# Attention through 32 landmarks with a two-layer feed-forward, one core: a shared PSUM slot for two output tiles, an earlier w_out load, and a first softmax by halves

## The chip, the core and the metric

The kernel runs on one core of a Trainium2 chip. The core has engines that run their own instruction streams side by side and wait for each other through semaphores: PE (TensorE, matmuls into the accumulation memory PSUM), ACT (ScalarE, functions of one tensor), DVE (VectorE, elementwise work), POOL (GpSimd, here used to start loads) and SP (SyncE, here used to start stores and transposing transfers). Sixteen DMA engines move the data. The metric is the device time of one execution in microseconds (us), as the median of several runs.

## The reference

For 8 batches of 8 heads, 576 tokens and 64 channels, a set of 32 landmark queries p first attends to k and v. The 32 results then serve as both keys and values for the 576 queries q. The outputs of the heads are joined to rows of 512, multiplied by w_in (512 x 2048), passed through a smooth ReLU, and multiplied by w_out (2048 x 512).

```python
def sm_attn(qq, kk, vv):
    s = scale * qq @ kk.T
    a = exp(s - max(s));  a = a / (sum(a) + 1e-9)
    return a @ vv
p_packed = sm_attn(p, k, v)                 # 32 x 64 for each head
x = join_heads(sm_attn(q, p_packed, p_packed))   # 4608 x 512
h = x @ w_in
g = where(h >= 1, h, where(h <= -1, 0, (h + 1)**2 / 4))
out = g @ w_out
```

## The kernel before

Loads cast float32 to bf16 on the way. Each batch b goes through these steps, named as the tiles are in the profile:

- k and q are turned (`tp`, `kT`, `qT`): in batches 0 and 1 by PE with copies out of PSUM, in later batches by transposing transfers that SP starts. The landmarks p are turned by PE (`tpp`, `pT`), for batches 2 to 7 in one step.
- PE multiplies landmarks with k (`sp`), ACT takes the exponent (`ex`), PE multiplies with v (`pk`), and the result is copied (`ppT`). From batch 2 on DVE first copies v into `vz`.
- PE multiplies the packed keys with q (`s`), ACT takes the exponent (`eT`), PE sums over the landmarks (`sm`), ACT makes the reciprocal as logarithm and exponent (`ln`, `rc`), and DVE scales (`A`). The eight heads go as two groups of four (`G = 2`).
- The packed values are multiplied with w_in at once (`mp`, copied to `M`, in four parts of 512 columns), so that a tile of the hidden layer (`h`, 128 of the 2048 columns, all 576 tokens as two halves) is four matmuls of M with A.
- The smooth ReLU of an h tile is three steps: `x` on ACT, `t` on DVE or ACT, `hT` on DVE.
- Two batches make a pair of 1152 tokens, which is nine output tiles of 128 tokens. An output tile (`o`) sums sixteen matmuls, one for each h tile; it is copied to `ob` by ACT or DVE and stored by SP.

The order of everything is made when the program is built. Each step is a `Task` with a rank, the engines that may run it with assumed durations, what it depends on, and what buffers it takes. `Plan.run` plays the tasks against these durations and always takes the step that can start first (within a slack, the one of the lowest rank); the instructions are emitted in that order, and on the chip each engine keeps to it. So a rank or an assumed duration that changes moves instructions on all engines.

PSUM holds three slots of two banks (buffer `w`, pool `psW`), through which nearly all tiles pass, and two slots of one bank (buffer `o`, pool `psO`) for output tiles. In the first pair of batches output tiles 2 and 5 borrow a `w` slot each (`LENT`). Until the first output matmul, gaps that the plan foresees on PE are filled with matmuls on zeros (`o<-zeros`, `warm`, line 866).

The loads of w_in and w_out come in quarters (`win0` to `win3`, `wout0` to `wout3`), in the order of `LOADS`. `wout0` is needed by the first four matmuls of every output tile. k and v of batches 2 to 7 each have one buffer (`kz`, `v`), so a batch's load waits until the batch before has used it.

Of the kernel before, what the change touches and what calls it, by code (L numbers as in the profile page):

```python
# [11 lines left out]
class Task:  # L12
# [4 lines left out]
    def __init__(self, rank, ways, deps=(), takes=(), mode=None, behind=()):  # L17
        self.rank, self.ways, self.deps = rank, ways, list(deps)
        self.behind = [d for d in behind if d is not None]
        self.takes, self.frees, self.mode = list(takes), [], mode  # L20
        self.start = self.end = self.engine = None
        self.users = []


class Plan:
# [7 lines left out]
    def __init__(self, buffers):  # L33
        self.tasks = []
# [5 lines left out]
    def add(self, rank, ways, deps=(), takes=(), mode=None, behind=()):  # L40
        t = Task(rank, ways, deps, takes, mode, behind)
        self.tasks.append(t)
        return t
# [7 lines left out]
    def run(self, slack):  # L51
# [6 lines left out]
        while ready:  # L58
            best = None
            found = defaultdict(list)  # L60
            left = {b: sorted(v) for b, v in self.slots.items()}
            for t in sorted(ready, key=lambda t: t.rank):
                at = max((d.end + self.LATENCY for d in t.deps), default=0.0)
                at = max([at] + [d.start + 0.001 for d in t.behind])
                need = defaultdict(int)
                for b in t.takes:
                    need[b] += 1
                short = any(len(left[b]) < n for b, n in need.items())
                wants = at < self.free["PE"] + self.CLAIM
                for b, n in need.items():  # L70
                    if not short:
                        at = max(at, left[b][n - 1] + self.LATENCY)
                    if wants:
                        del left[b][:n]
                if short:
                    continue
                for e in t.ways:
                    found[e].append((max(self.free[e], at), t))
            for e, some in found.items():
                first = min(x[0] for x in some)  # L80
                at, t = min((x for x in some if x[0] <= first + slack.get(e, 0.0)), key=lambda x: (x[1].rank, x[0]))
                if best is None or at < best[0]:
                    best = at, t, e
# [38 lines left out]
def kernel(  # L122
# [20 lines left out]
    P = 128  # L143
# [16 lines left out]
    XSPLIT = 0  # L160
    FROM, C5, R5 = 2, 5, 64
    PAIRED = 2
    SPLIT, AHALF, WPARTS, MPARTS, QLATE, ORDER3, ORDER, MERGE = 2, 0, 1, 2, 0, 4, 2, 2
    Q0 = [range(0, 8, 2), range(1, 5, 2), range(5, 9, 2)]
    LOADS = "k0 v0 q0 win0 win1 win2 k1 wout0 v1 wout1 win3 wout2 q1 wout3 q2 v2 k2 p"
# [3 lines left out]
    LENT = [2, 5]  # L169
# [22 lines left out]
    plan = Plan(dict(BUFS, dma=8))  # L192
# [64 lines left out]
    def dma(key, rank, emit, mb, takes=(), settle=0.9):  # L257
        t = plan.add(rank, {"DMA": (0.78, 2.1, emit, mb / 0.405, settle)}, takes=list(takes) + ["dma"])
# [22 lines left out]
    def load_five(nm, b, rank):  # L281

        for i, (c, p0, t0) in enumerate([(C5, 0, 0), (C5 - 1, R5, C5 * R5)]):
            def emit(e, c=c, p0=p0, t0=t0):
                of = {"k": k, "v": v}[nm][b, :, t0:t0 + R5 * c].rearrange("h (p c) d -> p h (c d)", c=c)
                G_.dma_start(tokens(nm, b)[p0:p0 + R5, :, :c * D], of)  # L286
            dma((nm, b, i), rank + 0.01 * i, emit, 1.3 * c / 9, [nm] if i == 0 else [], 0.9 if b < 2 else 1.7)
# [4 lines left out]
    def load(nm, b, rank):  # L292

        if five(nm, b):
            load_five(nm, b, rank)
            return
        for i, hs in enumerate({("k", 0): [range(4, 8)], ("q", 0): Q0}.get((nm, b), [range(H)])):
            def emit(e, hs=hs):
                G_.dma_start(tokens(nm, b)[:, heads(hs)], rows_of(nm, b, hs))  # L299
            mb = MB0.get((nm, b, hs[0]), (1.18 if b < 2 else 1.3) * len(hs) / H)  # L300
# [601 lines left out]
```

## Time and profile before

| what | value |
|---|---|
| runs (us) | 243.82, 243.79, 244.25; median 243.82 |
| profiled execution | 244.38 us, of which the span is 242.6 us |
| busy in the span | PE 236.0, ACT 196.0, DVE 176.4, weight loads 134.5, POOL 36.2 us |
| granted PE clock | full in every slice |
| moved by DMA | 36.24 MB, mean 149 GB/s |

The span runs from the first to the last instruction of the profiled execution; its own time has 1.78 us around that. A busy PE counts matmuls as they overlap, so it says that PE had no gap, not that it ran at its peak. A group row ends with the idle time of the engine just before the group and what ended it. A timeline row gives the start, the length, the engine, the line, the operation and the number of instructions that are merged into it. A row on DMA gives the queue, the size and the time from issue to landing.

### The profile page before, as it was taken

The numbers are of one execution on the slowest core, as the hardware profiler recorded it, in microseconds if no ns is written. First come the engines' busy times: TensorE is split into PE (matmuls) and PEld (weight loads), VectorE is DVE, ScalarE is ACT, GpSimd is POOL, SyncE is SP. The second block draws the span as 40 slices with busy tenths as digits, with TensorE's granted clock in tenths as the row PEclk, the third lists the DMA queues.
The fourth block names the chain that finished last, engine by engine and source line by source line (L and its number), as shares of the span: only waits on it lengthen the run. The fifth ranks groups of instructions, "written<-read, shape, count | busy, mean of one in ns | idle before, by whom it ended". The sixth has DMA issues, their size and how long they took to land.

```text
span 242.6 us, 5421 instructions
## 1 busy us (share of the span) xinstructions
PE 236.0 (97%) x2160; PEld 134.5 (55%) x2160; DVE 176.4 (73%) x307; ACT 196.0 (81%) x329; POOL 36.2 (15%) x54
## 2 busy tenths in 40 slices
PE   7899999999999999999999999999999999999993
PEld 2645656465555655466546655665565555555452
DVE  4557987479967995799859986986798797775000
ACT  3587986999979994999899899989999998885111
POOL 8562141000070005006003300400000000000000
PEclk9999999999999999999999999999999999999999
DMA  7999999999579999999999998991941111122223
GB/s 163 192 206 205 206 206 204 201 158 176 147 91 221 212 169 182 230 211 143 220 215 187 161 219 162 152 219 48 193 98 47 47 43 43 46 63 68 60 73 87
DMA packets 63994, 36.24 MB, mean 149 GB/s; under 512 B 33632, under 2 KB 59488, under 8 KB 63968
## 3 DMA queue, kind: packets, MB, share of 16 engines
q0 software_dynamic: 27520, 18.25, 52.6%
q1 hardware_dynamic: 35744, 17.08, 32.4%
q10 hardware_dynamic: 704, 0.56, 0.8%
q8 instruction: 17, 0.28, 0.5%
q14 instruction: 9, 0.07, 0.1%
HBM read 37.22 MB, written 9.44 MB: 192 GB/s over the span
## 4 chain that ended last, share of the span: by engine, by line
PE 91%; DMA 4%; ACT 2%; POOL 1%; issue 1%; ACTq 0%; POOLq 0%
PE o L798 52%; PE h L724 25%; DMA q<-in_q_dram 4%; PE mp L591 3%; PE sm L633 2%; PE o L866 2%; PE tp L401 1%; PE pk L538 1%; PE sp L460 1%; PE s L578 1%; ACT x L730 1%; PE pk L548 1%; ACT t L740 0%; PE sp L475 0%; PE pk L543 0%
## 5 line engine op out<-in xcount | busy, mean ns | idle before, releaser
L798 PE MATMUL o<-w_out_sb,hT 128*128 128x512 bf16 (+1 forms) x592 | 146.7, 374 | 0.0
L745 DVE SCALAR_TENSOR_TENSOR hT<-t 128x576 bf16<-128x576 f32 (+1 forms) x130 | 93.9, 745 | 8.9 <-ACT t L740 7.1
L730 ACT ACTIVATE x<-h 128x576 f32<-128x576 f32 (+1 forms) x130 | 79.4, 661 | 10.1 <-PE h L724 8.8
L798 PEld LDWEIGHTS <-hT 128*128 128x128 bf16 x592 | 55.5, 98 | 50.3 <-issue 5.6
L724 PE MATMUL h<-A,M 128*128 128x288 bf16 x512 | 78.8, 286 | 0.5 <-ACT x L730 0.5
L724 PEld LDWEIGHTS <-M 128*128 128x128 bf16 x512 | 49.3, 98 | 27.1 <-issue 1.4
L740 ACT ACTIVATE t<-x 128x576 f32<-128x576 f32 (+1 forms) x65 | 44.9, 698 | 0.9
L738 DVE TENSOR_SCALAR t<-x 128x576 f32<-128x576 f32 (+1 forms) x65 | 29.9, 461 | 7.5 <-ACT x L730 7.0
L200 ACT COPY ob<-o 128x512 f32<-128x512 f32 (+1 forms) x18 | 10.5, 582 | 14.1 <-PE o L798 14.1
L200 ACT CAST M<-mp 128x1024 bf16<-128x1024 f32 (+1 forms) x21 | 19.6, 973 | 1.2 <-PE mp L591 0.9
L286 POOL DMA_DIRECT2D kz<-in_k_dram x12 | 8.6, 723 | 68.6 <-DMA kT<-kz 67.5
L200 DVE COPY ob<-o 128x512 f32<-128x512 f32 x19 | 13.1, 688 | 7.9 <-PE o L798 7.1
L649 DVE SCALAR_TENSOR_TENSOR A<-eT,rs,rc 128x576 bf16<-128x576 bf16 x16 | 12.6, 816 | 8.3 <-ACT rc L644 8.3
L200 DVE CAST M<-mp 128x1024 bf16<-128x1024 f32 (+1 forms) x13 | 14.8, 1138 | 4.9 <-PE mp L591 4.9
L866 PE MATMUL o<-zeros 128*128 128x512 bf16 (+1 forms) x44 | 12.6, 404 | 1.2 <-DVE zeros L233 1.2
L286 POOL DMA_DIRECT2D v<-in_v_dram x12 | 8.4, 716 | 34.6 <-DVE vz L516 28.7
L626 ACT ACTIVATE eT<-s,rs 128x576 bf16<-128x576 f32 x16 | 11.0, 740 | 1.9 <-PE s L578 1.5
L482 ACT ACTIVATE ex<-sp 128x640 bf16<-128x640 f32 x12 | 8.1, 701 | 3.9 <-PE sp L460 3.9
L591 PE MATMUL mp<-w_in_sb,ppT 64*32 64x512 bf16 x256 | 10.8, 380 | 0.0
L639 ACT ACTIVATE ln<-sm 128x576 f32<-128x576 f32 x16 | 10.3, 648 | 0.4
L644 ACT ACTIVATE rc<-ln 128x576 f32<-128x576 f32 x16 | 10.3, 677 | 0.2
L299 POOL DMA_DIRECT2D q<-in_q_dram x10 | 8.0, 810 | 6.0 <-DMA k<-in_k_dram 2.9
(58 smaller groups left out, 115.6 us busy)
## 6 DMA issues: line engine op xcount, KB each, us to landing
out_dram<-ob SPq DMA_DIRECT2D x23, 192.0 KB, 2.4
q<-in_q_dram POOLq DMA_DIRECT2D x7, 576.0 KB, 13.7
out_dram<-ob SPq DMA_DIRECT2D x24, 128.0 KB, 3.2
w_out_sb<-in_moe_w_out_dram POOLq DMA_DIRECT2D x4, 512.0 KB, 19.6
v<-in_v_dram POOLq DMA_DIRECT2D x6, 320.0 KB, 9.4
kz<-in_k_dram POOLq DMA_DIRECT2D x6, 320.0 KB, 6.5
w_in_sb<-in_moe_w_in_dram POOLq DMA_DIRECT2D x3, 512.0 KB, 13.7
v<-in_v_dram POOLq DMA_DIRECT2D x6, 256.0 KB, 10.5
```

What stands on the lines that cost most here:

```text
L200: i = (nc.vector.tensor_copy if e == "DVE" else nc.scalar.copy)(to, of)
L286: G_.dma_start(tokens(nm, b)[p0:p0 + R5, :, :c * D], of)
L591: i = nc.tensor.matmul(have["mp", b, f][a * NP:(a + 1) * NP, g], have["ppT", b][r, g, a], w_in_sb[r, a, f * FW:(f + 1) * FW], start=True, ...
L626: nc.scalar.activation(have["eT", b, g][:, part], have["s2", b, g][:, part, :HALF], AF.Exp, scale=rs_of[b][:, g, 1:])
L649: V.scalar_tensor_tensor(have["A", b][:, g, part], have["eT", b, g][:, part], rs_of[b][:, g, :1], have["rc", b, g][:, part], ALU.mult, ALU ...
L724: nc.tensor.matmul(have["h", b, fi][:, hf, :HALF], have["M", b][:, g, fi * P:(fi + 1) * P], have["A", b][:, g, hf], start=(g == 0), stop=( ...
L730: nc.scalar.activation(have["x", b, fi][:, hs[0]:hs[-1] + 1], have["h", b, fi][:, hs[0]:hs[-1] + 1, :HALF], AF.Prelu, bias=-1.0, alpha=0.5)
L738: V.tensor_scalar(t, x, 1.0, 0.0, ALU.add, ALU.max)
L740: nc.scalar.activation(t, x, AF.Relu, bias=1.0)
L745: V.scalar_tensor_tensor(dst, t, 1.0, t, ALU.min, ALU.mult)
L798: nc.tensor.matmul(have["o", key][:, :w], hT[:, fi, i * P:(i + 1) * P], w_out_sb[:, fi, cols], start=(fi == 0), stop=(fi == KF - 1))
L866: nc.tensor.matmul(o[:, :w], zeros[:, :P], zeros[:, :w], start=True, stop=True)
```

## The change

1. Output tiles 2 and 3 of the first pair share one `w` slot, one bank each (`SHARED`). Tile 3 had a `psO` slot of its own; tile 5 goes on borrowing a slot alone.
2. `LOADS`: `wout0` comes behind `win1`; then `win2`, `win3`, `wout1`, and only then k and v of batch 1. `LATER` writes out the order of q, k and v for batches 3 to 7.
3. `XSPLIT = 1`: in batch 0 the second softmax goes by halves of the tokens, each step once for each half.
4. Steps get names, and `MOVES` shifts the rank of some thirty of them.
5. The planner's rules and assumed durations: when no step can start because a waiting one has claimed its buffers, it now looks again without claims; transfers of later batches are assumed shorter, and so are stores.

```diff
-    XSPLIT = 0
+    XSPLIT = 1
-    LOADS = "k0 v0 q0 win0 win1 win2 k1 wout0 v1 wout1 win3 wout2 q1 wout3 q2 v2 k2 p"
+    LOADS = "k0 v0 q0 win0 win1 wout0 win2 win3 wout1 k1 v1 wout2 q1 wout3 q2 v2 k2 p"
+    LATER = "v3 k3 q3 q4 k4 v4 q5 k5 v5 k6 v6 q6 q7 k7 v7"
+    MOVES = {"ex5.1": (0.6, 0), "h0.11": (10.9, 0), "h0.12": (8.9, 0), "h0.14": (13.8, 0), "h0.15": (6.9, 0),
...
-    LENT = [2, 5]
+    LENT = [5]
+    SHARED = [(2, 3)]
...
+        move, stretch = self.moves.get(name, (0.0, 0.0))
+        first = self.first.setdefault(name, rank)
+        t = Task(rank + move + stretch * (rank - first), ways, deps, takes, mode, behind, name)
...
+            for claims in (True, False):
...
+                    wants = claims and at < self.free["PE"] + self.CLAIM
...
+                if best is not None:
+                    break
...
-                    self.pipe = max(self.pipe, at + 1.5) + t.ways[e][3] * (1.4 if beside else 1.0)
+                    self.pipe = max(self.pipe, at + 1.5) + t.ways[e][3] * (1.1 if beside else 1.0)
...
-            dma((nm, b, i), rank + 0.01 * i, emit, 1.3 * c / 9, [nm] if i == 0 else [], 0.9 if b < 2 else 1.7)
+            dma((nm, b, i), rank + 0.01 * i, emit, 1.2 * c / 9, [nm] if i == 0 else [], 0.9 if b < 2 else 1.4, hold)
...
                 for nm, t in zip("eslra", (t_e, t_s, t_l, t_r, t_a)):
+                    t.behind.extend(steps.get((nm, g), []))
                     steps.setdefault((nm, g), []).append(t)
...
+        both = next((x for x in SHARED if pr == 0 and i in x), None)
...
-                    if fi == 0:
+                    if fi == 0 and both:
+                        if i == both[0]:
+                            have["o2", both] = wide([P, 2 * FW], f32, "o")
+                        have["o", key] = have["o2", both][:, both.index(i) * FW:][:, :d_model]
+                    elif fi == 0:
...
+            if both:
+                copied.setdefault(both, []).append(c)
+                if i == both[1]:
+                    plan.release("w", copied[both])
+            else:
+                plan.release("w" if lent else "o", [c])
...
-            st = plan.add(last + 0.01, {"SP": (0.4 * len(rows), 3.0, store, 0.9 / parts, 0.0)}, [c])
+            st = plan.add(last + 0.01, {"SP": (0.4 * len(rows), 3.0, store, 0.75 / parts, 0.0)}, [c], name=f"o{pr}.{i}")
```

Three places of the two programs' orders follow, with the lines of each program's own file. On POOL, the loads that follow q of batch 0, before and then after. A quarter of w_in is 128x4x512 (the first one comes as two of 64 partitions), a quarter of w_out as well; k, v and q of batch 1 are 96x8x384.

```order
L310 DMA w_in_sb<-in_moe_w_in_dram 64x4x512 x2
L310 DMA w_in_sb<-in_moe_w_in_dram 128x4x512 x2
L299 DMA k<-in_k_dram 96x8x384
L315 DMA w_out_sb<-in_moe_w_out_dram 128x4x512
L299 DMA v<-in_v_dram 96x8x384
L315 DMA w_out_sb<-in_moe_w_out_dram 128x4x512
L310 DMA w_in_sb<-in_moe_w_in_dram 128x4x512
```

```order
L330 DMA w_in_sb<-in_moe_w_in_dram 64x4x512 x2
L330 DMA w_in_sb<-in_moe_w_in_dram 128x4x512
L335 DMA w_out_sb<-in_moe_w_out_dram 128x4x512
L330 DMA w_in_sb<-in_moe_w_in_dram 128x4x512 x2
L335 DMA w_out_sb<-in_moe_w_out_dram 128x4x512
L319 DMA k<-in_k_dram 96x8x384
L319 DMA v<-in_v_dram 96x8x384
```

The first quarter of w_out takes the third quarter of w_in's place, and k and v of batch 1 move back behind three loads of weights.

On ACT, the first batch's second softmax, from the copies of `qT` to the first `x`, before and then after:

```order
L200 COPY qT<-tp 128x288 x2
L626 ACTIVATE eT<-s_325,rs 128x576
L626 ACTIVATE eT<-s_340,rs 128x576
L639 ACTIVATE ln<-sm 128x576 x2
L644 ACTIVATE rc<-ln 128x576 x2
L200 CAST M<-mp 128x512
L730 ACTIVATE x<-h 128x288 x2
```

```order
L213 COPY qT<-tp 128x288
L646 ACTIVATE eT<-s_314,rs 128x288 x2
L659 ACTIVATE ln<-sm 128x288
L646 ACTIVATE eT<-s_346,rs 128x288 x2
L659 ACTIVATE ln<-sm 128x288
L664 ACTIVATE rc<-ln 128x288 x2
L659 ACTIVATE ln<-sm 128x288
L213 CAST M<-mp 128x512
L664 ACTIVATE rc<-ln 128x288
L659 ACTIVATE ln<-sm 128x288
L664 ACTIVATE rc<-ln 128x288
L751 ACTIVATE x<-h 128x288 x2
```

Six activations of 576 tokens become twelve of 288. On PE the scores of the first group now stand ahead of the last six transposes of q.

On SP, from the last load of the start to the third batch's transposes (kT and qT of batch 2), before and then after. A store of one output tile is two instructions here (its rows lie in two places of the output).

```order
L342 DMA k_raw<-in_k_dram 96x2x384
L816 DMA out_dram<-ob 96x512
L816 DMA out_dram<-ob 32x512
L434 DMA_TRANSPOSE kT<-kz 128x20x128
L434 DMA_TRANSPOSE qT<-q 128x24x96
```

```order
L362 DMA k_raw<-in_k_dram 96x2x384
L851 DMA out_dram<-ob 96x512
L851 DMA out_dram<-ob 32x512
L851 DMA out_dram<-ob 64x512 x2
L851 DMA out_dram<-ob 32x512
L851 DMA out_dram<-ob 96x512
L454 DMA_TRANSPOSE kT<-kz 128x20x128
L454 DMA_TRANSPOSE qT<-q 128x24x96
```

Three output tiles are stored ahead of the transposes, not one. Later in the program the scores of batches 3 to 7 also stand elsewhere among the output matmuls: ahead of batch 3's there are 149 output matmuls, not 160, with 48 h tiles in both.

More of the change, by code (lines that the diff above doesn't have):

```diff
@@ L59, in run @@
             best = None
[L60 to L83, printed above, removed]
+            for claims in (True, False):
+                found = defaultdict(list)
+                left = {b: sorted(v) for b, v in self.slots.items()}
+                for t in sorted(ready, key=lambda t: t.rank):
+                    at = max((d.end + self.LATENCY for d in t.deps), default=0.0)
+                    at = max([at] + [d.start + 0.001 for d in t.behind])
+                    need = defaultdict(int)
+                    for b in t.takes:
+                        need[b] += 1
+                    short = any(len(left[b]) < n for b, n in need.items())
+                    wants = claims and at < self.free["PE"] + self.CLAIM
+                    for b, n in need.items():
+                        if not short:
+                            at = max(at, left[b][n - 1] + self.LATENCY)
+                        if wants:
+                            del left[b][:n]
+                    if short:
+                        continue
+                    for e in t.ways:
+                        found[e].append((max(self.free[e], at), t))
+                for e, some in found.items():
+                    first = min(x[0] for x in some)
+                    at, t = min((x for x in some if x[0] <= first + slack.get(e, 0.0)), key=lambda x: (x[1].rank, x[0]))
+                    if best is None or at < best[0]:
+                        best = at, t, e
+                if best is not None:
+                    break
@@ L255, in chain, with dma, held @@
         return t
-    def dma(key, rank, emit, mb, takes=(), settle=0.9):
-        t = plan.add(rank, {"DMA": (0.78, 2.1, emit, mb / 0.405, settle)}, takes=list(takes) + ["dma"])
+    def dma(key, rank, emit, mb, takes=(), settle=0.9, hold=()):
+        def held(e):
+            t.made = emit(e)
+            for h in hold:
+                tc.add_manual_dep(t.made.ins, h.made.ins.name, mybir.DependencyInfo(
+                    mybir.DependencyClass.Sync, mybir.DependencyReason.DATA), reason="a load begun behind another has landed")
+        t = plan.add(rank, {"DMA": (0.78, 2.1, held, mb / 0.405, settle)}, hold, takes=list(takes) + ["dma"])
         plan.release("dma", [t])
@@ L329 @@
             load(what[0], int(what[1]), -1000 + n)
-    for b in range(3, B):
-        for n, nm in enumerate(["kqv", "kvq", "qkv", "qvk", "vkq", "vqk"][ORDER3 if b == 3 else ORDER]):
-            load(nm, b, -960 + 10 * b + n)
+    for n, what in enumerate(LATER.split()):
+        what, *other = what.split("@")
+        load(what[0], int(what[1]), -930 + n, [t for o in other for t in landed[o[0], int(o[1]), 0 if o[0] == "q" else 7]])
     def load_p_raw(e):
```

87 lines of the change are left out of this document (44 added, 43 removed), and 5 rows, old and new, of the table MOVES.

## The prediction

> **What bounds the kernel now.** I read the page's head and its chain first, then a table of windows, then the PE timeline from 16 to 28 us.
>
> ```profile
> span 242.6 us, 5421 instructions
> PE 236.0 (97%) x2160; PEld 134.5 (55%) x2160; DVE 176.4 (73%) x307; ACT 196.0 (81%) x329; POOL 36.2 (15%) x54
> PE 91%; DMA 4%; ACT 2%; POOL 1%; issue 1%; ACTq 0%; POOLq 0%
> 12.04:27.80 15.76, 15.19 (x172) 8.81 (x173) 11.52 (x24) 13.41 (x29) 6.11 (x8) 1.00 1.27 205
> 27.80:43.15 15.35, 15.35 (x182) 8.72 (x178) 12.83 (x24) 12.78 (x21) 3.64 (x5) 1.00 1.27 206
> 55.40:65.90 10.50, 10.47 (x85) 5.96 (x85) 10.21 (x18) 10.16 (x17) 0.00 (x0) 1.00 0.90 170
> 92.08:238.80 146.72, 146.72 (x1263) 83.99 (x1261) 105.47 (x173) 119.77 (x198) 12.85 (x18) 1.00 0.71 130
> ```
>
> The window rows give length, then busy time of PE, weight loads, DVE, ACT, POOL, then clock, DMA share and GB/s. PE is the bound from 27.8 us on: it is busy 15.35 of 15.35 us there and 146.72 of 146.72 us later. The changed kernel issues the same useful matmuls, so the end moves only by what PE loses before its useful work closes up, and by any new wait after that. The loss before is here (the first two rows are the fillers in the window 12.0 to 27.8):
>
> ```profile
> L866 PE MATMUL o<-zeros 128*128 128x512 bf16 x18 | 5.4, 382 | 0.0
> L866 PE MATMUL o<-zeros 128*128 128x256 bf16 x6 | 1.6, 272 | 0.0
> 17.29 2.01 PE L866 MATMUL o<-zeros 128*128 128x512 bf16 x9
> 19.14 0.65 PE L724 MATMUL h<-A,M 128*128 128x288 bf16 x4
> 24.77 0.65 PE L724 MATMUL h<-A,M 128*128 128x288 bf16 x4 [0.48 <-ACT x L730]
> 27.80 1.24 PE L798 MATMUL o<-w_out_sb,hT 128*128 128x512 bf16 x5
> 76.85 0.98 PE h L724 x8
> 89.01 3.24 PE o L798 x15
> ```
>
> The last two rows, of the chain, price a matmul: 0.122 us for an h (a tile is four, 0.49 us) and 0.216 us for an o. A full filler is as long as an o. The program of before fills 16 filler units (a half counts half) between the first scores and the first h tile, and 5 between that and the first o.
>
> **The change part by part.** *Fillers.* The changed program has 37 fillers, not 44: 11.5 units up to the first h and 3.5 from there to the first o. That is 6 units x 0.216 = 1.3 us less, if no wait takes their place.
>
> *Softmax by halves.* Its chain on ACT and DVE:
>
> ```profile
> 14.33 1.38 ACT L626 ACTIVATE eT<-s,rs 128x576 bf16<-128x576 f32 x2
> 16.75 1.25 ACT L644 ACTIVATE rc<-ln 128x576 f32<-128x576 f32 x2
> 17.46 1.55 DVE L649 SCALAR_TENSOR_TENSOR A<-eT,rs,rc 128x576 bf16<-128x576 bf16 x2 [0.22 <-ACT rc L644]
> L730 ACT ACTIVATE x<-h 128x576 f32<-128x576 f32 x5 | 3.1, 687 | 0.3 <-PE h L724 0.3
> L730 ACT ACTIVATE x<-h 128x288 f32<-128x288 f32 x4 | 1.4, 418 | 1.4 <-PE h L724 1.4
> ```
>
> A now ends at 19.01, and the first h starts at 19.14. Two halves take 2 x 418 against 687 ns where they stand alone, so six steps cut in two cost ACT up to 0.9 us. Against it, the first group's scores no longer stand behind the last six q transposes, and the first h needs only ten of the twelve ACT halves. I take the first h 0.3 us earlier; the ends are 0.6 (the 4.5 filler units, 0.97 us, less a wait of 0.4) and 0 (ACT has nothing to give).
>
> *w_out's first quarter.* POOL's issues (start, length of the issue) and the times to landing of single loads:
>
> ```profile
> 5.71 2.83 POOL L310 DMA_DIRECT2D w_in_sb<-in_moe_w_in_dram  x4
> w_in_sb<-in_moe_w_in_dram POOLq DMA_DIRECT2D x1, 512.0 KB, 13.7
> 12.27 0.76 POOL L315 DMA_DIRECT2D w_out_sb<-in_moe_w_out_dram  x1 [0.38 <-DMA q<-in_q_dram]
> w_out_sb<-in_moe_w_out_dram POOLq DMA_DIRECT2D x1, 512.0 KB, 14.7
> ```
>
> The fourth w_in issue, at 7.8, lands at 21.5; w_out's quarter lands at 27.0, just ahead of the first o. It takes that fourth place, so o's may run from 21.5 on, and two tiles in one slot let four tiles grow at once. Between 19.14 and 27.80 PE spends 8.66 us on 6.5 us of useful work (8 h tiles at 0.49, two M groups, k transposes and scores of batch 1). The changed order puts o's there: 1.5 filler units less (0.32), the 0.48 wait gone, and about 0.35 of short waits on PSUM slots: 1.15 us. k and v of batch 1 move back three loads, some 7 us by the 5.5 us between those two landings; k then lands near 32, and PE reaches it near 33. I count one new wait of 0.25 us for h's that come faster than ACT. Early part: -0.3 - 1.15 + 0.25 = **-1.2**, ends -1.6 and -0.5.
>
> *Batch 1's h tiles.* Nine more o's stand ahead of batch 1's second scores (45, not 36), 1.94 us. With -1.2 those scores run 0.75 us later by the clock, while 91 o's and 32 h tiles stand ahead of batch 2's scores as before. ACT and DVE must do sixteen tiles in 1.95 us less. In 55.40:65.90 they are busy 10.16 and 10.21 of 10.50 us. The slack lies earlier, and two ACT copies and one DVE copy of output tiles move ahead of that stretch (some 0.6 us each). I take **+0.5**; ends 0 and 1.2.
>
> *Landmarks of later batches.* Now the order puts three output tiles' stores on SP before the transposes of batch 2, where one stood:
>
> ```profile
> 45.59 0.81 SPq L816 DMA_DIRECT2D out_dram<-ob  x2
> out_dram<-ob SPq DMA_DIRECT2D x1, 192.0 KB, 5.0
> 43.00:54.00 11.00, 11.00 (x91) 5.89 (x90) 6.16 (x11) 10.12 (x17) 0.00 (x0) 1.00 1.31 180
> 38.08 0.91 POOL L318 DMA_DIRECT2D p_nat<-in_p_dram  x1 [2.14 <-DMA w_out_sb<-in_moe_w_out_dram]
> p_nat<-in_p_dram POOLq DMA_DIRECT2D x1, 192.0 KB, 16.0
> 55.41 0.76 PE L360 MATMUL tpp<-ident,p_nat 32*128 32x32 bf16 x24
> ```
>
> The DMA engines are full (share 1.31), and the store issued at 45.59 landed at 50.6, ahead of p (38.08 + 16.0 = 54.1), which was issued before it. Two more tiles are 512 KB, at 180 to 205 GB/s up to 2.6 us. PE comes to the transposes of p after 0.44 us more work, less 0.9 of gain: 55.0. p lands between 54.1 and 56.7; I take the middle, 55.4, because the third store is issued too late to pass whole: **+0.4**, ends 0 and 1.6. ACT and DVE wait there with PE, as their copies of it stand in order.
>
> The Trainium skill, "DMA: Bandwidth & Descriptors", section "Queues, rings and completion order", says that each DMA engine takes the queues with work in turn, packet by packet. By it both extra tiles pass ahead of p, which would make this term 1.6 instead of 0.4 and the sum 245.3. The trace shows one store passing, so it agrees in kind and cannot tell how much of three would pass.
>
> *Batch 3's kT.*
>
> ```profile
> 67.68 1.35 POOL L286 DMA_DIRECT2D v<-in_v_dram  x2 [28.69 <-DVE vz L516]
> 79.55 7.09 SPq L434 DMA_TRANSPOSE kT<-kz  x1
> kT<-kz SPq DMA_TRANSPOSE x1, 10.8
> 92.08 0.75 PE L460 MATMUL sp<-pT,kT 128*128 128x64 bf16 x20
> 69.60:88.20 18.60, 18.60 (x156) 10.71 (x154) 16.52 (x29) 17.38 (x31) 2.34 (x4) 1.00 1.34 203
> ```
>
> The loads of batch 3 start when DVE's second vz copy frees v, at 67.68, and kT lands at 79.55 + 10.8 = 90.35, 22.67 us later; PE uses it 24.40 us after the start. The changed order has 58 o's between batch 2's and batch 3's scores, not 69: 11 x 0.216 = 2.37 us less, leaving 22.03. The same four loads, three tiles of stores and transpose pass through full engines (203 GB/s), so PE waits 0.64. I take **+0.6**; ends 0 (stores outside the stretch) and 1.1 (the vz copy, one hT further back in DVE's order). Batches 4 and 5 hang on the same chain of load and transpose, each started by the kT before it; I count no wait of theirs, as fewer stores stand between their loads and their transposes than before. The edits of ranks, names and the planner's costs issue nothing and cost nothing by themselves. The tail after PE's last matmul is the same program.
>
> **Sum.** -1.2 + 0.5 + 0.4 + 0.6 = +0.3. The profiled execution took 244.38 us, 1.78 around its span; it lies 0.56 above the median 243.82. 244.38 + 0.3 = 244.7, so 244.1 as a median.
>
> **Rivals.** *The late waits do not come* (stores pass behind p, and kT lands with less ahead of it): -1.2 + 0.5 = -0.7, **243.1**, with ACT and DVE at their best end 242.6. For it speaks that PE never waited for kT or p before; against it, that kT had only 1.7 us to spare and loses 2.4.
>
> *Slower: the stores push p back whole.* Place: PE's transposes of p near 55. Price 1.6 instead of 0.4, and nothing after recovers it, since kT's chain starts from a DVE copy behind the same step: +1.5, **245.3**. It decides once p lands after 55.6. For it speaks the store that overtook p; against it, that a store takes 5.0 us to land and the third is issued near 50.
>
> *The change does not do what it says*: h and o come earlier but ACT, at 13.41 of 15.76 us already, cannot feed them, and PE idles where fillers ran. The early part is then -0.4 and the later waits nearly vanish with it: **243.7**.
>
> **Numbers.** 0.2% of this time, 0.49 us, is about what a measurement here can tell from no change. The forecast (gain paid back, 243.4 to 244.4) has 0.37; late waits absent 0.32; stores push p back 0.25; no early gain 0.06. Faster 0.33: the second case, and a little of the first's lower end. Slower 0.28: the third and the first's upper end. Same 0.39. The range 242.6 to 245.2 runs from the second case's best end to just short of the third's point, leaving about one in ten on each side.
>
> **What would show it.** Right: the first o near 22.5; fillers 37; the first PE waits named by DMA at tpp near 55 and at sp near 89; kT of batch 3 landing about 22.5 us after v's load. Wrong: PE fully busy from 23 us on (then 243.1 or less); p landing before 55 or after 56; a wait for k, v or w_out between 24 and 45, of which I expect none; a first h later than 19.1.

## The result, and the profile after

The changed kernel takes 249.66 us (median of 4 runs, 248.99 to 249.90), against 243.96 us for the kernel before (4 runs). The ratio is 1.0228, with an interval of 1.0205 to 1.0251: slower by 5.7 us, outside the predicted range. Times are medians; one execution, of the run that loads v earlier, fell in a slower state of the chip and is left out of its median. The profiled execution took 249.72 us, 5.34 more than that of before. From the profile's page of the changed kernel, the span, the fillers and the chain (the work that ended last, followed back from the last instruction):

```profile
span 247.9 us, 5411 instructions
...
L901 PE MATMUL o<-zeros 128*128 128x512 bf16 (+1 forms) x37 | 12.2, 446 | 1.2 <-DVE zeros L246 1.2
...
PE 71%; DMA 20%; DVE 3%; POOL 2%; ACT 2%; issue 1%; POOLq 0%; DVEq 0%
```

The chain was 91% PE and 4% DMA; now DMA holds 20% of it. The loss shows when the span is cut at the same five events in both kernels: batch 1's scores `s`, the landmark scores `sp` of batches 2, 3, 4 and 5, and the end of PE. The windows of the changed kernel (length, then PE's busy time first, the granted clock third from the end):

```profile
43.82:65.88 22.06, 20.66 (x172) 11.92 (x172) 18.34 (x31) 20.27 (x33) 0.00 (x0) 1.00 1.09 174
65.88:90.61 24.73, 24.03 (x225) 13.82 (x224) 20.35 (x38) 22.17 (x39) 4.26 (x6) 1.00 1.06 165
90.61:109.39 18.78, 18.75 (x191) 10.86 (x192) 13.36 (x24) 16.51 (x29) 3.50 (x5) 1.00 1.21 202
109.39:127.53 18.14, 15.66 (x171) 8.87 (x170) 15.49 (x27) 14.78 (x26) 5.84 (x8) 0.97 1.14 188
127.53:244.20 116.67, 116.63 (x914) 66.25 (x912) 79.76 (x126) 90.96 (x150) 4.67 (x7) 0.99 0.55 105
```

and the first and the fourth of the same windows of the kernel before:

```profile
43.15:65.87 22.72, 22.69 (x180) 12.47 (x180) 17.59 (x30) 21.50 (x35) 0.00 (x0) 1.00 1.10 176
...
114.78:138.21 23.43, 23.43 (x222) 13.68 (x221) 19.22 (x33) 21.16 (x36) 4.09 (x5) 1.00 1.15 194
```

Length less busy is PE's idle time: 1.40, 0.70, 0.03, 2.48 and 0.04 us after, 4.65 in all; before, 0.03. Up to batch 1's scores the change had gained: they come 0.67 us later on the clock, but nine more o's (1.94 us) are done by then, so 1.27 us. The rest of the loss is the clock, below 1.00 in the last two rows. It falls in one place, right behind the longest idle time:

```profile
120.00:126.00 6.00, 3.52 (x24) 2.08 (x23) 4.20 (x7) 3.12 (x5) 1.02 (x2) 1.00 1.13 196
126.00:130.00 4.00, 4.00 (x26) 2.38 (x25) 3.51 (x6) 3.87 (x7) 3.46 (x5) 0.57 1.01 164
```

Four us at 0.57 cost 4 x 0.43 = 1.72 us of full-rate work. The sum: -1.27 + 4.62 + 1.72 = 5.07 of the 5.34 us. What happens at 122 us, in timeline rows of POOL, DVE and PE, and the landing of v's second part:

```profile
109.55 1.59 POOL L306 DMA_DIRECT2D kz<-in_k_dram  x2 [14.93 <-DMA kT<-kz]
111.10 1.73 POOL L306 DMA_DIRECT2D v<-in_v_dram  x2
...
121.77 0.89 DVE L536 COPY vz<-v 128x2048 bf16<-128x2048 bf16 x2 [2.47 <-DMA v<-in_v_dram]
122.58 1.53 DVE L669 SCALAR_TENSOR_TENSOR A<-eT,rs,rc 128x576 bf16<-128x576 bf16 x2
124.03 1.21 DVE L213 CAST M<-mp 128x1024 bf16<-128x1024 f32 x1
...
122.16 0.65 PE L745 MATMUL h<-A,M 128*128 128x288 bf16 x4
125.30 2.01 PE L745 MATMUL h<-A,M 128*128 128x288 bf16 x12 [2.48 <-DVE M L213]
```

```profile
v<-in_v_dram POOLq DMA_DIRECT2D x1, 256.0 KB, 9.5
```

Read it backwards. PE waits 2.48 us for M. M's copy stands on DVE behind A (both of batch 4), and A behind the `vz` copies of batch 5, which waited 2.47 us for v of batch 5. v was started at 111.10, behind k, whose load waited for the kT of batch 4 to land. Nothing of batch 5 is needed yet; DVE only takes its steps in order. The trace names DVE as the releaser, yet what is waited for is a load two steps up. In the kernel before, no `vz` copy waits at all, and batch 5's first one stands behind batch 4's A and M:

```profile
124.16 1.54 DVE L649 SCALAR_TENSOR_TENSOR A<-eT,rs,rc 128x576 bf16<-128x576 bf16 x2
125.61 1.22 DVE L200 CAST M<-mp 128x1024 bf16<-128x1024 f32 x1
...
130.09 0.69 DVE L516 COPY vz<-v 128x2048 bf16<-128x2048 bf16 x1
```

v of batch 5 is no later than before: its second part lands at 112.14 + 9.5 = 121.7 us, before at 112.02 + 11.0 = 123.0. What moved is the copy. In the changed order 41 o's and 10 h tiles fewer stand ahead of the second step of batch 5's landmark scores (233 and 68, not 274 and 78), 13.8 us of PE work. A wait of DVE is not a loss by itself: batch 4's first `vz` copy waits 1.93 us at 103.17, and PE idles 0.03 us in the whole window 90.61:109.39.

### The profile page after: what moved, and what is told of

It is laid out like the page before. It is cut to its first block, busy times and chain, and to the rows that moved or that the text cites. A ratio compares the mean times of both kernels' runs of the same rounds, so it can differ in the third digit from the quotient of the medians.

```text
span 247.9 us, 5411 instructions
## 1 busy us (share of the span) xinstructions
PE 237.4 (96%) x2153; PEld 135.0 (54%) x2153; DVE 179.6 (72%) x309; ACT 196.6 (79%) x335; POOL 36.0 (15%) x54
## 4 chain that ended last, share of the span: by engine, by line
PE 71%; DMA 20%; DVE 3%; POOL 2%; ACT 2%; issue 1%; POOLq 0%; DVEq 0%
PE o L827 40%; PE h L745 19%; DMA kT<-kz 8%; DMA p_nat<-in_p_dram 6%; DMA v<-in_v_dram 4%; PE mp L611 3%; DMA k_raw<-in_k_dram 2%; PE o L901 2%; PE sp L480 1%; PE sm L653 1%; PE pk L558 1%; POOL kz L306 1%; PE s L598 1%; DVE M L213 1%; POOL v L306 1%; PE tp L421 1%
## 5 line engine op out<-in xcount | busy, mean ns | idle before, releaser
L761 ACT ACTIVATE t<-x 128x576 f32<-128x576 f32 (+1 forms) x69 | 46.9, 685 | 1.2
L759 DVE TENSOR_SCALAR t<-x 128x576 f32<-128x576 f32 (+1 forms) x61 | 27.7, 455 | 4.8 <-ACT x L751 4.5
L213 DVE CAST M<-mp 128x1024 bf16<-128x1024 f32 (+1 forms) x16 | 18.5, 1154 | 4.1 <-PE mp L611 4.0
L213 ACT COPY ob<-o 128x512 f32<-128x512 f32 (+1 forms) x17 | 9.6, 563 | 14.6 <-PE o L827 14.4
L213 ACT CAST M<-mp 128x1024 bf16<-128x1024 f32 (+1 forms) x18 | 16.6, 967 | 2.9 <-PE mp L611 2.9
L213 DVE COPY ob<-o 128x512 f32<-128x512 f32 x20 | 13.8, 688 | 6.7 <-PE o L827 6.4
L669 DVE SCALAR_TENSOR_TENSOR A<-eT,rs,rc 128x576 bf16<-128x576 bf16 (+1 forms) x18 | 12.8, 746 | 5.2 <-ACT rc L664 5.1
L646 ACT ACTIVATE eT<-s,rs 128x576 bf16<-128x576 f32 (+1 forms) x18 | 11.4, 684 | 2.0 <-PE s L598 1.8
L659 ACT ACTIVATE ln<-sm 128x576 f32<-128x576 f32 (+1 forms) x18 | 10.7, 600 | 0.6
L611 PE MATMUL mp<-w_in_sb,ppT 64*32 64x512 bf16 x256 | 10.7, 380 | 0.1
L664 ACT ACTIVATE rc<-ln 128x576 f32<-128x576 f32 (+1 forms) x18 | 10.4, 627 | 0.0
L536 DVE COPY vz<-v 128x2048 bf16<-128x2048 bf16 (+1 forms) x12 | 5.5, 483 | 4.8 <-DMA v<-in_v_dram 4.8
```

The lines of the kernel that those rows point to most:

```text
L213: i = (nc.vector.tensor_copy if e == "DVE" else nc.scalar.copy)(to, of)
L611: i = nc.tensor.matmul(have["mp", b, f][a * NP:(a + 1) * NP, g], have["ppT", b][r, g, a], w_in_sb[r, a, f * FW:(f + 1) * FW], start=True, ...
L646: nc.scalar.activation(have["eT", b, g][:, part], have["s2", b, g][:, part, :HALF], AF.Exp, scale=rs_of[b][:, g, 1:])
L669: V.scalar_tensor_tensor(have["A", b][:, g, part], have["eT", b, g][:, part], rs_of[b][:, g, :1], have["rc", b, g][:, part], ALU.mult, ALU ...
L759: V.tensor_scalar(t, x, 1.0, 0.0, ALU.add, ALU.max)
L761: nc.scalar.activation(t, x, AF.Relu, bias=1.0)
```

## The experiments

Theory 1 is that reading: a copy that waits for v's load blocks DVE, PE runs dry, the clock falls, and the planner's new durations are what put the copy there. Its rivals are that ACT and DVE are the bound there anyway (theory 2) and that the new layout itself costs the time (theory 3); theory 4 is on p, theory 5 on full DMA engines, theories 6 to 8 on where the early gain goes. In the same sets of runs the kernel before had medians of 243.96 to 244.13 us.

### One batch's copies moved on DVE

DVE's order, the only difference to the changed kernel:

```diff
-L536 COPY vz<-v 128x8x4x64
-L536 COPY vz<-v 64x512
 L669 SCALAR_TENSOR_TENSOR A<-eT,rs,rc 128x576 x2
 L213 CAST M<-mp 128x2x512
+L536 COPY vz<-v 128x8x4x64
+L536 COPY vz<-v 64x512
```

> One edit in the changed kernel's order: DVE's two copies of batch 5's v into vz stand behind batch 4's two A steps and its last copy of M, not ahead of them; nothing else moves. Theory 1 (the copy waits 2.47 us for v's load, everything behind it in DVE's order waits with it, PE runs dry for 2.48 us at 122.8 and its granted clock then falls): the wait of PE at that place goes, the clock stays full, and of the 3.1 us lost between 109 and 127.5 us and the further 1.0 us up to the end nearly all comes back: 245.6 to 246.6 us. Rival, theory 2 (ACT and DVE are the bound in this stretch, so the wait for v only covers work that is late anyway): less than 1 us comes back, 248.7 us or more.

Measured: 247.61 us (ratio 1.0157, 1.0108 to 1.0206), 2.05 less than the changed kernel. The wait at 122 is gone, but 3.1 to 4.1 were expected back. (Three executions took 247.2 to 247.9 us; the fourth took 249.85, with a mean clock of 0.991.) The timeline shows the same thing one batch later:

```profile
138.14 0.89 DVE L536 COPY vz<-v 128x2048 bf16<-128x2048 bf16 x2 [2.69 <-DMA v<-in_v_dram]
...
142.94 1.14 PE L745 MATMUL h<-A,M 128*128 128x288 bf16 x8 [2.03 <-DVE M L213]
```

In the changed kernel the delay at 122 hid this: its copy of batch 6's v starts at 139.44, when v had landed at 136.1. Here DVE is free for it at 135.45, and v lands at 138.05. So that pair was moved too (the same diff, for batch 6's copies behind batch 5's A and M).

> As the run in which batch 5's vz copies stand behind batch 4's A and M on DVE, with batch 6's two vz copies put behind batch 5's A and last copy of M as well. In that run the same wait came one batch later (DVE waits 2.69 us for v of batch 6 up to 138.1, PE waits 2.03 us for M up to 142.9). Theory 1: this wait goes too, no PE wait over 0.6 us is left behind 95 us, and the time is 247.6 less 2.0 to 2.7: 244.9 to 245.6 us, the level of the kernel with the old durations. Rival, theory 2 (ACT and DVE are late anyway, the wait takes another name): 246.9 us or more.

Measured: 246.26 us (1.0078, 1.0052 to 1.0104). From 109 us to the end the profile names no wait of PE over 0.4 us. The level is 0.7 above what was expected, but 3.40 of the 5.7 us hang on four copies on DVE that take 1.8 us in all. Theory 2 falls as the cause of these 3.40 us.

### The clock apart from the wait

The wait for M stays, and PE gets something to do in it:

```diff
+        if t is later:          # batch 4's first h tile
+            idle_work(11)       # matmul(growing o, zeros, zeros, start=False, stop=False)
         t.ways[t.engine][2](t.engine)
```

> Eleven matmuls on zeros (11 x 0.216 = 2.4 us) are put into PE's order where the changed kernel's PE waits at 122.8 us; they add zero to an output tile that is still growing. The wait for M stays. If the fall of the granted clock to 0.50 at 126 to 130 us follows from PE's idle time, the clock stays full in every run; the time falls by 0.7 us (as the one run of the changed kernel that kept its clock was shorter by that) up to 1.7 us (0.7% of 247.9): 248.0 to 249.0 us. Rival (the clock falls for another reason, such as the load on the chip): the clock falls as before, 249.7 us, or a little more where the fillers push the h tiles back.

Measured: 247.96 us (1.0148, 1.0125 to 1.0172), 1.70 less. Two rows of the timeline and the window in which the clock had been 0.57:

```profile
123.04 2.54 PE L909 MATMUL o<-zeros 128*128 128x512 bf16 x11
126.03 1.63 PE L745 MATMUL h<-A,M 128*128 128x288 bf16 x12 [0.46 <-DVE M L213]
```

```profile
126.00:130.00 4.00, 3.97 (x43) 2.83 (x43) 3.93 (x7) 3.28 (x6) 2.93 (x5) 1.00 0.99 197
```

The wait for M ends no sooner than in the changed kernel, the clock stays full in all four executions, and 1.7 us are back, the upper end of what was expected. So the fall of the clock follows from PE's idle time. Its price is known less well. The one execution of the changed kernel that kept its clock took 248.99 us, 0.7 less than the median of the other three; in the two runs below that leave out the step t, with the same fall, the one execution that kept its clock was shorter by 1.8 and 1.9 us.

### The planner's durations

The changed kernel with the old assumed durations, and with a single one of them (lines shortened; the loads of q change alike):

```diff
-    self.pipe = max(self.pipe, at + 1.5) + t.ways[e][3] * (1.1 if beside else 1.0)
+    self.pipe = max(self.pipe, at + 1.5) + t.ways[e][3] * (1.4 if beside else 1.0)
...
-    emit, 1.2 * c / 9, [nm] if i == 0 else [], 0.9 if b < 2 else 1.4, hold
+    emit, 1.3 * c / 9, [nm] if i == 0 else [], 0.9 if b < 2 else 1.7, hold
...
-    store, 0.75 / parts
+    store, 0.9 / parts
```

> The changed kernel with the planner's assumed durations of before (loads of later batches 1.3 and 1.7, transposes beside other work 1.4, stores 0.9); all the rest of the change stays. The order of PE is the same up to the transposes of p, and behind them batch 5's scores stand 8.8 us of PE work later than in the changed kernel. Theory 1 (the assumed shorter loads bring batch 5's attention ahead of its v): the loss behind 95 us vanishes and only the wait for p and part of the wait for batch 3's kT remain: 244.0 to 245.3 us, no wait of vz longer than 0.5 us in front of A. Rival, theory 3 (the shared slot, the load order and the halved softmax cost the time themselves): 247 us or more.

Measured: 245.70 us (1.0055, 1.0036 to 1.0074); no `vz` copy waits for v. The time is 0.4 above the expected range, and 3.96 us are back with the layout, the loads' order, the softmax and the ranks untouched. Then only the first of the three edits, the one on transposes:

> The changed kernel with one assumed duration put back: a transpose beside other transfers counts 1.4 times again, not 1.1; loads and stores stay assumed shorter. PE's order then has batch 4's scores 6.3 us and batch 5's 5.6 us of PE work later than the changed kernel, and DVE's vz copies for batches 4 and 5 stand behind A and M of the batch before. Theory 1: no copy of M or A waits for v of batch 5, the clock stays full, 245.3 to 246.5 us. Rival (the assumed loads matter as much): DVE waits for a later v in front of A, 247.5 us or more.

Measured: 244.99 us (1.0035, 1.0022 to 1.0048), 4.67 less than the changed kernel and 0.3 below the expected range. One number, which issues no instruction, makes most of the loss; the other two edits do no harm beside it here, as putting them back too gave no more. Its first and fourth window, cut as above:

```profile
43.56:65.21 21.65, 20.64 (x171) 11.91 (x171) 18.26 (x31) 20.26 (x33) 0.00 (x0) 1.00 1.10 180
...
113.72:129.85 16.13, 15.79 (x174) 9.02 (x173) 13.53 (x23) 14.10 (x26) 2.42 (x4) 1.00 1.25 200
```

The fourth has 0.34 us of idle time instead of 2.48. The first still has 1.01. The other way round, the kernel before with nothing but the new durations (the three edits reversed):

> The kernel before with nothing but the planner's new assumed durations (later loads 1.2 and 1.4, transposes beside other work 1.1, stores 0.75). Layout, load order and softmax are those of before; the planner's order brings batch 3's scores forward by 10.7 us of PE work and batch 4's by 13.8, and puts DVE's vz copies of later batches ahead of A and M. Theory 1: DVE waits for v in front of A or M, PE runs dry, and the kernel is slower by 2 to 6 us: 246 to 250 us. Rival, theory 3 (the durations do harm only together with the early part): within 1 us of before, 243.5 to 245 us.

Measured: 251.57 us (1.0285, 1.0249 to 1.0321), slower than expected, by the same mechanism at batch 4's copy:

```profile
96.02 0.69 DVE L516 COPY vz<-v 128x2048 bf16<-128x2048 bf16 x1 [7.87 <-DMA v<-in_v_dram]
...
99.55 0.88 PE L724 MATMUL h<-A,M 128*128 128x288 bf16 x3 [5.27 <-DVE M L200]
```

Without the early part the durations do even more harm. Theory 3 falls as the main cause: with all the rest of the change in place 0.35 to 0.55% are left. Which part of the rest costs that (layout, ranks, the order of later loads, the rule on claims) was not taken apart.

### Loading v earlier does not help

Only POOL's queue changes:

```diff
+    for b in (5, 6, 7):
+        ahead((f"load v.{b}.0", f"load v.{b}.1"), f"load k.{b}.0")
```

> The changed kernel with the orders of PE, ACT, DVE and SP untouched; on POOL alone v of batches 5, 6 and 7 is loaded ahead of k of the same batch. In the changed kernel k's load waits for the landing of the kT before (109.55) and v stands behind it (111.1), lands at 121.6. Theory 1 (v is late because its load is queued behind a load that waits for a transpose): v of batch 5 starts near 104.5, when DVE has copied v of batch 4, and lands before 115; DVE waits for no v from there on, PE's clock stays full, 245.0 to 246.2 us. Rival, theory 5 (the DMA engines are full here, so v's earlier load makes kT late by as much): PE waits for kT at sp of batch 5 or 6 instead, 247.5 us or more.

Measured: 254.19 us (1.0409, 1.0364 to 1.0454), the slowest of all. No copy waits for v of batch 5 any more. PE waits instead for batch 4's q, whose transpose was issued at the same time as v's load (106.88):

```profile
107.03 5.04 SPq L455 DMA_TRANSPOSE qT<-q  x1
...
120.68 0.68 PE L599 MATMUL s<-qT,ppT 64*32 64x288 bf16 x16 [5.02 <-DMA qT<-q]
```

The landing of that transpose, in this run and then in the changed kernel:

```profile
qT<-q SPq DMA_TRANSPOSE x1, 13.5
```

```profile
qT<-q SPq DMA_TRANSPOSE x1, 5.0
```

Theory 5 had the right kind of cause and the wrong victim: the transpose took 13.5 us to land, where the changed kernel needs qT at 115.39 and does not wait. PE idles 5.02 us, and the clock falls again (0.66 on average from 116 to 126 us). Brought forward in this way, v's load takes the time of a transpose that is needed sooner; what helped was to move the copies or the attention back.

### Where the early gain goes

p moved ahead of v and k of batch 2 on POOL's queue:

```diff
+    put(("p",), "load q.2.0")
```

> One edit in the changed kernel's order: on POOL's queue the load of p stands right behind q of batch 2, ahead of v and k of batch 2. In the changed kernel v's load starts at 38.42 us, released by batch 1's last pk matmul, and p behind it at 41.17; before it was 38.08. Theory 4 (p is late because it is queued behind a load that waits for PE): p is issued near 25.5 and lands before 42, PE no longer waits for it at 53.8, and 1.0 to 1.4 us come back: 248.2 to 248.7 us. Rival (ACT and DVE set the pace from 44 to 66 us, so that the wait for p only stands in place of another): less than 0.4 us, 249.3 us or more.

Measured: 249.45 us (1.0225, 1.0190 to 1.0261), no gain. p was there early, and PE waits as long, for hT:

```profile
27.52 0.91 POOL L339 DMA_DIRECT2D p_nat<-in_p_dram  x1 [1.37 <-DMA w_in_sb<-in_moe_w_in_dram]
...
53.31 0.60 PE L828 MATMUL o<-w_out_sb,hT 128*128 128x512 bf16 x2 [0.64 <-DVE hT L767]
...
55.02 1.04 PE L828 MATMUL o<-w_out_sb,hT 128*128 128x512 bf16 x4 [0.61 <-DVE hT L767]
55.98 0.76 PE L381 MATMUL tpp<-ident,p_nat 32*128 32x32 bf16 x24
```

Next the other side was relieved, alone and together with p (`cut` returns at once for batch 1, fi < 8, with `t` set to `x`):

> The changed kernel with the step t left out for batch 1's first eight h tiles (hT is made of x directly, so these eight tiles are not the reference's); every order is the same otherwise. ACT and DVE have 0.70 or 0.45 us less work for each of them between 50 and 58 us, p is loaded as late as in the changed kernel (issue 41.2, landing 55.8). If ACT and DVE alone made PE wait 1.2 us at 52 to 56 us, the wait is gone and batch 2's scores come 1.0 us sooner, near 64.9; if p alone did, PE waits for p until 55.8 as before and batch 2's scores stay near 65.8. Theory 7 (both end at the same time, so that either alone keeps PE waiting): PE reaches the transposes of p near 54.5 and waits 1.2 us for p; 249.2 to 249.7 us.

> The same with p loaded right behind q of batch 2 as well. Theory 7 (hT and p each hold PE up until 55.8): now nothing does, PE transposes p near 54.6 without waiting, batch 2's scores come near 64.7, 1.1 us sooner than in the changed kernel. The end moves less than that or as much, since the waits for kT of batch 3 and v of batches 4 and 5 hang on loads that start from DVE's copies: 248.2 to 249.2 us. Rival (the weak place is neither, but the order of PE): the transposes stay near 55.8.

Measured: 249.91 us (1.0230, 1.0203 to 1.0256), 0.2 above the expected range, and 249.20 us (1.0180, 1.0150 to 1.0209). With less for ACT and DVE, PE came to the transposes at 54.5 and waited for p; with both, it came at 55.3:

```profile
55.71 0.76 PE L380 MATMUL tpp<-ident,p_nat 32*128 32x32 bf16 x24 [1.17 <-DMA p_nat<-in_p_dram]
```

```profile
55.31 0.76 PE L381 MATMUL tpp<-ident,p_nat 32*128 32x32 bf16 x24
```

Either one alone holds PE until 55.7 to 56.0, so the first half of theory 7 stands. Taking both away brought 0.5 us, not 1.1: a wait of 0.44 us for hT was left.

Then the late part was exchanged: the planner's list, made with the old durations, is cut at a named step, and behind it stand the steps that are left, on the engines and in the order of the kernel before.

```diff
+    cut = next(i for i, t in enumerate(order) if t.name == "s1.0")   # or "sp2.0", "sp3.0"
+    order[cut:] = late
```

The cut at batch 1's scores:

> The changed kernel's order up to batch 1's scores (shared slot, early w_out, halved softmax, old durations), and from there on every engine takes the rest in the order of the kernel before. PE's order has no early attention and DVE's vz copies stand as before, so nothing of the late loss is left. Theory 6 (the early gain of 1.27 us is real, but ACT and DVE, which have idled 2 us more up to 44 us, cannot feed batch 1's h tiles 1.3 us earlier, and PE waits 1.0 to 1.3 us for hT near 54): 243.5 to 244.1 us, first h, first o and batch 1's scores as in the changed kernel. Rival (the wait near 54 is p's and the order of before hides it): 242.5 to 243.1 us. Rival (kT of batch 3 now comes late, with 2 us of stores moved): 244.6 us or more.

Measured: 246.87 us (1.0105, 1.0085 to 1.0124), in the last rival's range, but not for its cause: kT is not waited for. The o's that had run early are missing as cover for the chain of batch 1's softmax and M. Between batch 1's scores and its first h tile the order has 18 o's in the kernel before and in the changed one; here 6 are left:

```profile
49.92 0.65 PE L746 MATMUL h<-A,M 128*128 128x288 bf16 x4 [1.63 <-ACT M L213]
```

```profile
46.00:50.00 4.00, 1.67 (x21) 0.69 (x21) 1.80 (x3) 3.28 (x6) 0.00 (x0) 1.00 1.40 197
51.00:54.00 3.00, 3.00 (x14) 1.65 (x12) 2.39 (x4) 2.10 (x4) 0.00 (x0) 0.50 1.04 77
```

PE is busy 1.67 of 4 us, and the clock then falls to 0.50. The early gain is in part borrowed: o's done early are not there when PE needs them. The cut at batch 3's and at batch 2's landmark scores:

> The changed kernel with the old durations, in its own order up to batch 3's scores on landmarks; from there every engine takes the rest in the order of the kernel before. At that place the kernel with the old durations stood 0.7 us ahead of before (PE's clock time less the PE work done), and behind it lost 1.5 us in short waits for hT and DVE. If those belong to its order behind batch 3's scores: 243.0 to 243.7 us. Rival (the early lead is not kept, because kT of batch 4 and later loads do not come sooner): 243.8 to 244.5 us. Rival (as in the run that switched at batch 1's scores, the order of before finds something missing at the seam): 245 us or more.

> The same with the switch at batch 2's scores on landmarks, where the kernel with the old durations stood 1.15 us ahead of before by PE's work done. If the lead is kept: 242.8 to 243.4 us. Rival (kT of batch 3, which had 1.7 us to spare before, comes late because v of batch 2 starts only when PE has done batch 1's pk): PE waits for kT near 90 us, 243.8 us or more.

Measured: 244.96 us (1.0043, 1.0026 to 1.0061) and 244.31 us (1.0011, 1.0001 to 1.0020). With its own order kept up to 65 us and the order of before behind it, the change is worth nothing. In the profiled executions of the second one, 0.85 us of lead are left at batch 2's landmark scores (65.67 us with 94 o's ahead in the order, against 65.87 with 91) and 0.41 at batch 3's (91.67 against 92.08, 160 o's in both); in the medians nothing is left at the end. The leads of 0.7 and 1.15 us that the expectations start from were not kept, and PE waited for no kT, the rival's cause.

Two tries to take work out of the stretch from 50 to 58 us, both on the version at 244.31: p earlier, its transposes behind or ahead of batch 1's second M matmuls, all four copies on DVE.

> The kernel that switches to the order of before at batch 2's scores (244.3 us), with three moves: p is loaded ahead of q of batch 2, PE transposes it behind batch 1's second group of M matmuls (47.7 us) and no longer at 55.3, and DVE makes all four copies of it right behind batch 1's A, where it idles 1.0 us (ACT made two of them, 1.59 us, at 56.1). Theory 8 (the early gain is lost between 50 and 58 us, where ACT and DVE are busy throughout and p comes late): PE's waits of 0.34 and 0.32 us at 53 to 55 us shrink, batch 2's scores come 0.5 to 0.9 us sooner than 65.7, and the time is 243.4 to 243.9 us, faster than before by 0.1 to 0.3%. Rival (DVE's four copies, 2.26 us, now hold back the first hT of batch 1 by as much): 244.2 us or more.

> As the run with the landmarks moved early, but PE transposes p ahead of batch 1's second group of M matmuls (near 47.2 us) and p is loaded ahead of w_out's last quarter, so that it has landed. PE then needs no slot that M's copies hold: the 1.15 us wait at 47.9 goes. Theory 8 (ACT's and DVE's work between 50 and 58 us holds the early gain): batch 2's scores come 0.3 to 0.8 us sooner than in the run that switches to the order of before at batch 2 (65.7), 243.5 to 244.1 us. Rival (M's copies now come 0.7 us later, batch 1's h tiles start later by as much, and nothing is gained): 244.3 us or more.

Measured: 245.58 us (1.0056, 1.0039 to 1.0074) and 246.04 us (1.0072, 1.0060 to 1.0084). Both slower. One row of each:

```profile
49.02 0.75 PE L381 MATMUL tpp<-ident,p_nat 32*128 32x32 bf16 x24 [1.15 <-ACT M L213]
```

```profile
50.03 0.41 PE L612 MATMUL mp<-w_in_sb,ppT 64*32 64x512 bf16 x8 [1.13 <-ACT M L213]
```

Whichever of the two comes second waits 1.1 us until ACT has copied M out of its slot: no slot is free then for p's tile beside M's two. In the second run, w_out's last quarter, now behind p, is late as well: PE waits 0.55 us for it at 44.84. These runs don't say whether relief of ACT and DVE would bring the gain back; that stays open. No version here beats the kernel before.

## Why the prediction was wrong

**The early part, -1.2: right.** First h at 18.81 (0.33 earlier, 0.3 forecast), first o at 22.54 (22.5), 37 fillers, 1.27 us gained at batch 1's scores. In the changed kernel:

```profile
18.81 0.65 PE L745 MATMUL h<-A,M 128*128 128x288 bf16 x4
...
22.54 0.59 PE L827 MATMUL o<-w_out_sb,hT 128*128 128x512 bf16 x2
```

From 22.54 to 43.82 PE idled 0.21 us; 0.25 was forecast for the new wait. No k, v or w_out was waited for there.

**Batch 1's h tiles +0.5, p +0.4: mis-sized, and p's cause was another.** Forecast at 0.9 together, they measured 1.37 (1.40 us idle, less 0.03 before). Rows around p:

```profile
38.42 1.36 POOL L306 DMA_DIRECT2D v<-in_v_dram  x2 [12.98 <-PE pk L563]
...
41.17 0.92 POOL L338 DMA_DIRECT2D p_nat<-in_p_dram  x1
...
53.85 1.03 PE L827 MATMUL o<-w_out_sb,hT 128*128 128x512 bf16 x4
55.84 0.76 PE L380 MATMUL tpp<-ident,p_nat 32*128 32x32 bf16 x24 [0.96 <-DMA p_nat<-in_p_dram]
```

```profile
p_nat<-in_p_dram POOLq DMA_DIRECT2D x1, 192.0 KB, 14.6
```

p landed at 41.17 + 14.6 = 55.8, 0.4 later than forecast. But it took less time to land than before (14.6, not 16.0), beside six store issues on SP from 45.99 to 50.4 where two had stood, so the push by stores that the prediction priced does not show. It was issued 3.1 us later, because v of batch 2, ahead of it on POOL, waited for batch 1's last pk. That stands later in PE's order, with batch 1's landmark scores (34.96 us, not 26.96), as the planner expects k and v of batch 1 later; PE itself waited for neither. The prediction moved k and v back and did not follow their buffers to what is queued behind. The rule of the Trainium skill it weighed ("DMA: Bandwidth & Descriptors", "Queues, rings and completion order": queues with work are served in turn) put p's landing up to 2.6 us further behind its issue; in this run it came 1.4 us sooner after it, so that rule did not decide here. And p was not the price by itself: with p early PE waited as long for hT. The terms overlap; they do not add.

**Batch 3's kT, +0.6: right.** PE waited 0.70 us; v's load to kT's landing took 79.84 + 10.7 - 68.21 = 22.33 us (22.67 before). PE came to its place 21.70 us after that load, 0.3 sooner than the 22.03 of the sum; as both legs were 0.3 shorter, the two errors cancel.

```profile
68.21 1.35 POOL L306 DMA_DIRECT2D v<-in_v_dram  x2 [26.11 <-DVE vz L536]
...
79.84 6.97 SPq L454 DMA_TRANSPOSE kT<-kz  x1
...
90.61 0.76 PE L480 MATMUL sp<-pT,kT 128*128 128x64 bf16 x20 [0.70 <-DMA kT<-kz]
```

```profile
kT<-kz SPq DMA_TRANSPOSE x1, 10.7
```

**Batches 4 and 5, "I count no wait of theirs": wrong, and most of the miss (2.55 us of idle time behind 90.6 us, and the clock's 1.72).** For kT it held: PE waited for none after batch 3's. Three steps failed in it. It followed kT, and not v, which is loaded behind k from the same start. It looked for PE's own waits on a transfer; what waited was a DVE copy with other batches' work behind it. And it set the planner's durations at nothing because they issue nothing, while PE's order shows 13.8 us of work moved from ahead of batch 5's landmark scores to behind them, while v of batch 5 lands only 1.3 us sooner (121.7, not 123.0). Putting back one of the durations returns 4.67 us. The Trainium skill states the point that was missed: "PSUM — Partial Sum Buffer", section "Engine vs sequencer instructions", says that the queues of ScalarE, VectorE and GpSimd are strict first in, first out. The rows at 121.77 to 124.03 agree: A and M wait 2.47 us for a v that they don't read.

**The clock: not in the sum at all.** It fell after PE's idle time and cost some 1.7 us (0.7 to 1.9 by the comparisons above). The prediction priced no wait by what the clock does after it.

All signs that the prediction named for being right came true (the second wait at 90.6 us, not 89), and the total missed by 5.6 us: every sign lay ahead of 91 us, and most of the loss behind it. At 90.6 us the idle times sum to -1.27 + 1.37 + 0.70 = +0.80, where +0.3 was forecast; behind it come 2.55 + 1.72 = 4.27.

## What to carry to other kernels

An edit of a scheduler's assumed durations is a change to every engine's order: look up what now stands ahead of what on each in-order engine, and for each step that waits for a load, what is queued behind it that does not need that load. Where a transfer chain sets its own pace, work that is brought forward past it turns into a wait, and the profile names the engine that was blocked, not the load. A gap on PE is to be priced with the clock that falls behind it.

## What the hardware showed

- After 2.48 us without a matmul the granted clock went to 0.50 (single o's then took 0.41 and 0.43 us instead of 0.216) for 3.4 us; in one of four executions of the same program it stayed full. With p loaded early the gap was 2.91 us, and all four executions lost clock. A gap of 2.03 us (at 142.94, one batch's copies moved) left it full in the profiled execution. In the run that goes over to the order of before at batch 1's scores no gap was over 1.63 us, but PE was busy only 1.67 of 4 us, and it fell all the same. So the length of one gap does not decide alone. The Trainium skill, "TensorE: Matmul & The Clock Gate", section "HAM oscillation — how this bites in real kernels", puts the limit at gaps of about 3.4 us; these runs fell at shorter ones. Its section "What's actually happening" says that the window runs freely, by which the same gap may or may not cross it; the one execution in four that kept its clock fits that.
- In this kernel a load issued beside a transpose held that transpose up for longer than the load took: v's two parts landed 5.8 and 8.6 us after their issue, the transpose of q beside them only after 13.5, against 5.0 without them.
